# Linformer attention and an MLP mixer in one kernel: stores moved to GpSimd's queue, zero products in TensorE's early waits, another order of the first loads, and new turns between loads and DMA transposes

## The chip, the cores and the metric

The kernel runs on one core of one Trainium2 chip. The metric is the device time of one execution in microseconds (us); the smaller is the better. Before the change it was 439.4 us, the median of four runs (438.73 to 440.3 us). When the prediction was made, three of these were known, with a median of 438.74 us.

TensorE is the engine of the matrix products, VectorE (DVE in the profile) and ScalarE (ACT) do elementwise work, GpSimd (POOL) does elementwise work and issues DMAs, and SyncE (SP) only issues DMAs here.

## The reference, cut to what matters

```python
# batch 8, heads 8, sequence 1024, head width 64; E and F are 64 x 1024
k_proj = einsum('ks,bhsd->bhkd', E, k)
v_proj = einsum('ks,bhsd->bhkd', F, v)
attn   = softmax(q @ k_proj^T / 8)            # 1024 x 64 per head
x      = attn @ v_proj                        # then heads side by side: 8 x 1024 x 512
h      = relu(x^T @ w_tok1) @ w_tok2          # token mixing, 1024 -> 256 -> 1024
u      = x + h^T
out    = u + relu(u @ w_ch1) @ w_ch2          # channel mixing, 512 -> 1536 -> 512
```

Channel mixing is most of the work. The kernel does it with seven products of half-size blocks instead of eight, so it needs u transposed (called `uT`, two halves per batch: `uT0` and `uT1`), sums of blocks of `uT` (called `S`), and combinations of weight blocks (`wT`).

## The kernel before

The program gives every piece of work to a planner written in Python, as a job with an engine, an estimated duration, dependencies and a priority. The planner simulates the engines and lays down the order in which jobs are emitted. On the chip each engine then runs its jobs in that order and waits where an input is missing. The parts which the change and the argument touch follow; cuts are marked.

The start: the first batch's loads, pair of heads by pair of heads, with the two token-mixing weights near the end. All loads are issued by GpSimd, so they stand in one in-order queue.

```python
    for hp in range(HP):                       # HP = 4 pairs of heads
        if hp == HP - 1:
            ...
            ld(1.05, dma(wt1_sb, w1t), writes=["wt1"], prio=next(first))
        for name in "kvq":
            load_heads(0, name, 2 * hp, 2, next(first))
    ...
    ld(1.05, dma(wt2_sb, w2t), writes=["wt2"], prio=next(first))
    # ... then the channel weights, then batch 1
    for i in range(8):
        warm(i)                                # eight products of zeros, one per PSUM bank
```

The steady part: DMA transposes of q and u and all stores are issued by SyncE. The loads of the next batch are issued behind a transpose (`tie` makes one DMA wait for another), so that loads and transposes take turns.

```python
    def q_transpose(due):                      # qT <- q_sb, two DMA transposes on SyncE
        for h in range(0, H, H // 2):
            before = turned[0]
            turned[0] = sp(3.5, lambda h=h: nc.sync.dma_start_transpose(...), ...)
            if before:
                turned[0].deps.add(before)
    ...
            j = sp(3.5, lambda: nc.sync.dma_start_transpose(out=uT_t[i]..., in_=u_t[b % 2]...), ...)
            if landed[0]:
                tie(j, landed[0])              # uT waits for the last load issued
            turned[0] = j
    ...
        def store(sh):                         # two stores per block, sixteen blocks
            sp(1.5, lambda: nc.sync.dma_start(out=out_v[b, :, rows, :], in_=o_t[os[sh]]), ...)
    ...
    def load_batch(b):                         # k, v and q of batch b, all together
        jobs = [load_heads(b, n, hh, H // 2, None) for n in "kvq" for hh in range(0, H, H // 2)]
        for j in jobs if turned[0] else ():
            tie(j, turned[0])                  # behind the last transpose
        landed[0] = jobs[-1]
```

The softmax here doesn't subtract the row's maximum and nothing guards it: scores larger than these inputs give would overflow.

Of the kernel before, what the change touches and what calls it, by code (L numbers as in the profile page):

```python
# [10 lines left out]
BF16 = mybir.dt.bfloat16  # L11
ALU = mybir.AluOpType
ACT = mybir.ActivationFunctionType
FMAX = 3.4028234663852886e38


# [18 lines left out]
class Planner:  # L35
# [4 lines left out]
    def __init__(self, caps, homes):  # L40
        self.jobs, self.caps, self.homes = [], caps, homes
        self.wrote, self.readers = {}, {}

    def add(self, eng, occ, lat, fn, reads=(), writes=(), prio=None, takes=(), uses=(), after=()):
        j = Job(len(self.jobs), eng, occ, lat, fn, prio)
# [26 lines left out]
    def plan(self):  # L72
# [2 lines left out]
                d.next.append(j)  # L75
        for j in reversed(self.jobs):
            if j.prio is None:
                due = [s.prio for s in j.next]
                j.prio = (min(due) if due else 1e9) - j.occ - 0.3
        for j in self.jobs:  # L80
            if j.prio > 1e8:
                j.prio = max((d.prio for d in j.deps), default=0) + 2
# [3 lines left out]
        est = {}  # L86
# [39 lines left out]
        while any(can.values()):  # L126
            pick = None
            for e, js in can.items():
                f = free.get(e, 0.0)
                cands = []  # L130
                for j in js:
                    t = max(f, est[j.n])
                    spot = None
                    if j.takes:
                        h = home(j.takes[0], t)
                        if h is None:
                            continue
                        t, spot = h[0], h[3]
                    cands.append((t, j.prio, j.n, j, spot))
                if not cands:  # L140
                    continue
                t0 = min(c[0] for c in cands) + 0.02
                c = min((c for c in cands if c[0] <= t0), key=lambda c: (c[1], c[2]))
                if pick is None or c[0] < pick[0]:
                    pick = c
            if pick is None:
                raise RuntimeError("no job can go on", [(j.eng, j.fn.__qualname__, j.prio) for js in can.values() for j in js][:20], held, bank_free)
            t, _, _, j, spot = pick
            can[j.eng].remove(j)
            j.start, j.end, j.full = t, t + j.lat, t + j.lat + 0.03  # L150
            free[j.eng] = t + j.occ
            if j.takes:
                b = j.takes[0]
                b.at = spot
                turn[b.stream].remove(b)
                held[b.stream] += 1
                bank_free[spot] = None
            for b in j.banks:
                left[id(b)] -= 1
                if not left[id(b)]:  # L160
                    held[b.stream] -= 1
                    bank_free[b.at] = max(x.end for x in b.jobs) + 0.1
                    clean[b.at] = b.full
            order.append(j)
            for s in j.next:
                waiting[s.n] -= 1
                if not waiting[s.n]:
                    open_(s)
        assert len(order) == len(self.jobs), (len(order), len(self.jobs))
        return order  # L170


@with_exitstack
def kernel(
# [14 lines left out]
    P = 128  # L189
# [139 lines left out]
            writes=[(name, i) for i in range(h, h + hn)], prio=due,  # L329
        )  # L330
    first = iter(range(-1000, 0))
    for hp in range(HP):
        if hp == HP - 1:
            w1t = moe_w_tok1.rearrange("(p si) t -> p si t", p=P)
            ld(1.05, dma(wt1_sb, w1t), writes=["wt1"], prio=next(first))
        for name in "kvq":
            load_heads(0, name, 2 * hp, 2, next(first))
    w2t = moe_w_tok2.rearrange("(tc p) s -> p tc s", p=P)
    ld(1.05, dma(wt2_sb, w2t), writes=["wt2"], prio=next(first))
    w1_v = moe_w_ch1.rearrange("(dc p) (ch c) -> p dc ch c", p=P, ch=2)  # L340
    cw = DC // 2 // SETS
    for m in range(SETS):
# [32 lines left out]

    def blank(b):
        nc.tensor.matmul(  # L377
            b, zero, vb.rearrange("k h c d -> k (h c d)")[:, 0:S2], start=True, stop=True
        )

    def warm(i):
# [10 lines left out]
        make_identity(nc, ident)  # L392
        make_identity(nc, ident32)

    pl.add("POOL", 1.0, 1.0, identities, writes=["ident"], prio=-150)

    for n, (src, dst) in enumerate(((EF[0], ET_sb), (EF[1], FT_sb))):
        b = Bank("F", full=False)

        def view(b=b):  # L400
            return bank(b).rearrange("p (si k) -> p si k", si=NSI)

        def turn(src=src, view=view):
            for si in range(NSI):
                nc.tensor.transpose(view()[:, si, :], src[:, si:S:NSI], ident32)

        def take(dst=dst, view=view):
            nc.vector.tensor_copy(out=dst, in_=view())

        pl.add("PE", 1.6, 1.6, turn, reads=["ident"], takes=[b], prio=-150)  # L410
        dve(512, take, writes=["ET", "FT"][n : n + 1], uses=[b], prio=-150)

    def combine(T, b11, b12, b21, b22, cols, name, n, reads):
        def one(k, out, in0, in1, *deps):
# [93 lines left out]
            writes=[("kT", 1, h) for h in heads], uses=[bk],  # L508
        )

    turned = [None]
    landed = [None]

    def q_transpose(due):
        for h in range(0, H, H // 2):
            before = turned[0]
            turned[0] = sp(
                3.5,
                lambda h=h: nc.sync.dma_start_transpose(
                    out=qT[:, h : h + H // 2].rearrange("p h j s -> p (h j) s"),  # L520
                    in_=q_sb[:, h : h + H // 2].rearrange("p h si d -> p (h si d)"),
                ),
                reads=[("q", i) for i in range(h, h + H // 2)],
                writes=[("qT", i) for i in range(h, h + H // 2)], prio=due,
            )
            if before:
                turned[0].deps.add(before)

    def q_transpose_pe(hp, due):
        bk = Bank(stream[0], full=False)  # L530
# [93 lines left out]
    def token2(b, si, due):  # L624
# [20 lines left out]
        if si % NJ == NJ - 1:  # L645
            i = si // NJ
            j = sp(
                3.5,
                lambda: nc.sync.dma_start_transpose(
                    out=uT_t[i].rearrange("p s dc q -> p (s dc) q"),  # L650
                    in_=u_t[b % 2][:, i * NJ : (i + 1) * NJ].rearrange("p s d -> p (s d)"),
                ),
                reads=[("u", b % 2, n) for n in range(i * NJ, (i + 1) * NJ)],
                writes=[("uT", i, n) for n in range(HP)], prio=None,
            )
            if landed[0]:
                tie(j, landed[0])
            turned[0] = j

    def quarter(j, sh, dh):  # L660
        return uT_t[j % 2][:, 2 * sh : 2 * sh + 2, 2 * dh : 2 * dh + 2, :]
# [1 line left out]
    def s_sums(j):  # L663
        St = S_t[j % 2]
        a11, a12, a21, a22 = [quarter(j, sh, dh) for sh in range(2) for dh in range(2)]
        rd = [("uT", j % 2, n) for n in range(HP)]

        def one(n, in0, in1, add=False, deps=()):
            f = nc.vector.tensor_add if add else nc.vector.tensor_sub
            dve(  # L670
                512, lambda: f(out=St[:, n], in0=in0, in1=in1), ps=False,  # L671
                reads=rd + [("S", j % 2, m) for m in deps], writes=[("S", j % 2, n)],
            )

        one(0, a21, a22, add=True)
        one(2, a11, a21)
        one(1, St[:, 0], a11, deps=(0,))
        one(3, a12, St[:, 1], deps=(1,))

# [191 lines left out]
    def down_block(j):  # L871
# [30 lines left out]
        def product(n, i):  # L902
# [5 lines left out]
            for t in range(2):  # L908
# [5 lines left out]
                    prio=due_d(j, 2 * i + t),  # L914
                )

        def store(sh):
            rows = slice(i * NJ + 2 * sh, i * NJ + 2 * sh + 2)
            sp(
                1.5, lambda: nc.sync.dma_start(out=out_v[b, :, rows, :], in_=o_t[os[sh]]),  # L920
                reads=[o_key(sh, 0), o_key(sh, 1)], prio=None,
            )

# [52 lines left out]
            u_transpose_pe(hp, i, (-5.5 if i == 0 else 1.5) + 0.5 * hp)  # L976
    stream[0] = "F"

    def load_batch(b):
        jobs = [load_heads(b, n, hh, H // 2, None) for n in "kvq" for hh in range(0, H, H // 2)]  # L980
        for j in jobs if turned[0] else ():
            tie(j, turned[0])
        landed[0] = jobs[-1]

    def front(b, begin, end):
        units = []
# [5 lines left out]
        for i in range(H // hn):  # L992
            unit(1.9 * hn / H, lambda t, i=i: kv_proj(b, i * hn, hn, t))
            unit(0.9 * hn / H, lambda t, i=i: k_transpose(i * hn, hn, t))
            if b == 1:
                for hp in range(2 * i, 2 * i + 2):
                    unit(0.4, lambda t, hp=hp: q_transpose_pe(hp, t))
        unit(0.4, lambda t: scores(0, t))
        unit(0.4, lambda t: scores(1, t))
        for h in range(H):  # L1000
            if h + 2 < H:
                unit(0.4, lambda t, h=h: scores(h + 2, t))
            for half in range(2):
                unit(0.25, lambda t, h=h, half=half: attend(h, half, t))
        if b + 1 < B:
            unit(0.0, lambda t: load_batch(b + 1))
        for n in range(TC):
            unit(1.8, lambda t, n=n: token1(n, t))
        for si in range(NSI):
# [10 lines left out]
    for b in range(B):  # L1020
# [5 lines left out]
        if b + 1 < B:  # L1026
            at = 2 * TU * (b + 1)
            if b > 0:
                q_transpose(None)
            front(b + 1, at - 62, at - 14)  # L1030
    gate = mybir.DependencyInfo(mybir.DependencyClass.Sync, mybir.DependencyReason.DATA)
    plan = pl.plan()
    name_of = {}
    shown = None
    for j in plan:
        n = len(nc.cur_bb.bb.instructions)
        j.fn()
        new = nc.cur_bb.bb.instructions[n:]
# [35 lines left out]
```

## Time and profile before

| what | reading | view |
|---|---|---|
| device time | 439.4 us, median of 4 | times |
| span of the profiled execution | 439.5 us (its device time was 441.52 us) | page |
| TensorE busy | 418.5 us, 95% | page |
| TensorE idle, 45 to 420 us | 4.7 us | windows |
| TensorE at half pace | from 9.3 until about 22 us | timeline, spacing of equal products |
| DMA transpose of u, issue to landing | 4.3 / 4.6 / 7.2 us (min / median / max) | tile uT, 60 to 440 us |

The first lines are from the page of the kernel before: the busy times of the engines, and the shares of the chain that ended last.

```profile
PE 418.5 (95%) x3736; PEld 338.4 (77%) x3736; DVE 321.0 (73%) x783; ACT 241.1 (55%) x439; POOL 106.2 (24%) x122
PE 86%; DVE 7%; ACT 2%; DMA 2%; issue 1%; DVEq 0%; ACTq 0%
```

TensorE bounds this kernel: it is busy for 95% of the span and holds 86% of the chain.

The windows of the kernel before show it by stage. The columns are the stretch, its length, then the busy time and number of instructions of PE, PEld, DVE, ACT and POOL, the granted TensorE clock, the mean busy share of the DMA engines (it may exceed 1 where packets overlap), and GB/s.

```profile
0.00:22.90 22.90, 15.98 (x122) 10.16 (x122) 8.52 (x31) 8.84 (x17) 15.47 (x28) 1.00 1.08 188
22.90:45.00 22.10, 19.96 (x260) 17.20 (x261) 17.11 (x51) 14.39 (x30) 7.54 (x10) 1.00 1.31 203
45.00:165.00 120.00, 118.50 (x1075) 96.02 (x1074) 99.30 (x252) 72.60 (x132) 27.58 (x30) 1.00 0.86 155
165.00:420.00 255.00, 251.83 (x2178) 204.81 (x2177) 190.23 (x443) 141.41 (x255) 51.04 (x50) 1.00 0.62 123
420.00:439.50 19.50, 12.19 (x108) 10.24 (x105) 5.87 (x11) 3.84 (x7) 4.57 (x4) 0.97 0.27 108
```

From 45 to 420 us TensorE is idle for 1.5 + 3.2 us. The room is in the first 45 us, where the DMA engines are saturated (share above 1) and TensorE waits for data.

The next lines are TensorE's timeline of the kernel before: start, duration, engine, line, operation, output and inputs. They are two equal pairs of projection products at two moments, and the first product that needs the first batch's `uT` of the last pair of heads.

```profile
9.29 0.31 PE L455 MATMUL ps<-k_sb,ET_sb 128*64 128x128 bf16 x1
9.40 0.31 PE L455 MATMUL ps<-k_sb,ET_sb 128*64 128x128 bf16 x1
25.91 0.22 PE L455 MATMUL ps<-k_sb,ET_sb 128*64 128x128 bf16 x1
25.96 0.22 PE L455 MATMUL ps<-k_sb,ET_sb 128*64 128x128 bf16 x1
38.91 0.60 PE L801 MATMUL ps<-uT,wc_sb 128*128 128x256 bf16 x4
```

Equal products start 0.11 us apart at 9.3 us and 0.05 us apart at 25.9 us: early on TensorE runs at half pace. The clock column of the windows says 1.00 for that stretch, so it does not show this; the spacing of equal products does. The Trainium skill, "TensorE: Matmul & The Clock Gate", Part 1 (The HAM clock gate), has the mechanism: a gate lets half of the clock pulses through until TensorE has been active for a whole window of about 3.4 us. The trace agrees with the factor of two.

Last, three views of how u transposes fare in the kernel before: the waits in SyncE's queue (line, what it waited for, us in total, times, longest), the landing line of tile `uT`, and the one landing of a u transpose among the longest pieces of the chain (start, us, what).

```profile
SPq L920 <- POOL o L927: 189.0, 13, 67.4
SPq L649 <- DVE u L640: 62.4, 7, 18.2
```

```profile
DMA to landing us min/median/max: 4.3/4.6/7.2
```

```profile
269.21 7.15 DMA uT<-u
```

The stores (L920) wait in SyncE's queue for GpSimd's addition, and the transposes (L649) wait 62.4 us for u itself, which is as it should be; of their other waits, 43.5 us end with TensorE's products and 32.6 us with VectorE's G (lines not shown). Once issued, a transpose needs 4.3 to 7.2 us, and only one of them lies on the chain with its landing.

### The profile page before, as it was taken

How to read it: one execution, taken by the hardware profiler on the slowest of the kernel's cores; microseconds unless marked ns; L12 is line 12 of the kernel's file. 1: busy time of each engine (PE TensorE's matmuls, PEld its weight loads, DVE VectorE, ACT ScalarE, POOL GpSimd, SP SyncE). 2: the span in 40 equal slices, each digit the busy share in tenths (PEclk: the TensorE clock that was granted, in tenths of full speed). 3: DMA queues.
4: the chain of work that ended last, by engine and by line, in shares of the span. 5: the costliest groups of instructions: out<-in, count | busy, mean ns of one | idle time of the engine just before them, and what ended most of it. 6: DMA issues, size and time to landing. Idle time of an engine off the chain costs nothing.

```text
span 439.5 us, 9315 instructions
## 1 busy us (share of the span) xinstructions
PE 418.5 (95%) x3736; PEld 338.4 (77%) x3736; DVE 321.0 (73%) x783; ACT 241.1 (55%) x439; POOL 106.2 (24%) x122
## 2 busy tenths in 40 slices
PE   6789999999999999999999999899999999999993
PEld 4468888578778886788778877688768886888883
DVE  3459969678978797779697696778697596966451
ACT  1557786258536754567356654558436663555540
POOL 8442123032301331115021331115112210212212
PEclk9999999999999999999999999999999999999999
DMA  9999979289955899198955899187992811241022
GB/s 167 208 199 207 206 123 195 91 186 167 177 94 152 126 194 172 46 224 149 197 89 120 139 189 203 22 193 140 199 142 47 195 48 49 50 145 61 36 98 95
DMA packets 89516, 60.89 MB, mean 139 GB/s; under 512 B 55681, under 2 KB 84865, under 8 KB 89473
## 3 DMA queue, kind: packets, MB, share of 16 engines
q0 software_dynamic: 30624, 29.36, 42.7%
q1 hardware_dynamic: 58768, 30.68, 29.4%
q8 instruction: 29, 0.48, 0.4%
q10 hardware_dynamic: 80, 0.26, 0.3%
q14 instruction: 15, 0.11, 0.1%
HBM read 59.24 MB, written 16.78 MB: 173 GB/s over the span
## 4 chain that ended last, share of the span: by engine, by line
PE 86%; DVE 7%; ACT 2%; DMA 2%; issue 1%; DVEq 0%; ACTq 0%
PE ps L896 32%; PE ps L801 30%; PE ps L609 6%; PE ps L629 5%; PE ps L555 3%; PE ps L455 3%; PE ps L578 3%; DMA uT<-u 2%; DVE S L671 1%; DVE u L728 1%; PE ps L539 1%; ACT qT L547 1%; PE ps L377 1%; PE ps L689 1%; DVE da L943 1%
## 5 line engine op out<-in xcount | busy, mean ns | idle before, releaser
L896 PEld LDWEIGHTS <-G 128*128 128x128 bf16 x1344 | 130.0, 98 | 24.5 <-issue 5.7
L896 PE MATMUL ps<-wc_sb,G 128*128 128x256 bf16 x768 | 103.8, 273 | 3.9 <-DVE da L943 2.7
L801 PEld LDWEIGHTS <-wc_sb 128*128 128x128 bf16 x768 | 73.6, 98 | 14.3 <-issue 1.6
L823 ACT ACTIVATE G<-ps 128x512 bf16<-128x512 f32 x96 | 57.2, 599 | 39.9 <-PE ps L801 39.6
L896 PE MATMUL ps<-wT,G 128*128 128x256 bf16 x576 | 77.7, 272 | 0.1
L927 POOL TENSOR_TENSOR o<-o,u 128x512 f32<-128x512 f32 x32 | 37.4, 1169 | 130.3 <-ACT o L925 115.2
L801 PEld LDWEIGHTS <-wT 128*128 128x128 bf16 x576 | 55.1, 98 | 11.2 <-issue 2.2
L801 PE MATMUL ps<-uT,wc_sb 128*128 128x256 bf16 x384 | 57.6, 273 | 0.0
L801 PE MATMUL ps<-S,wc_sb 128*128 128x256 bf16 x384 | 57.6, 273 | 0.0
L927 POOL TENSOR_TENSOR db<-db,u 128x512 f32<-128x512 f32 x16 | 18.9, 1182 | 157.5 <-ACT db L925 157.5
L801 PE MATMUL ps<-S,wT 128*128 128x256 bf16 x384 | 54.9, 273 | 0.9 <-ACT G L823 0.7
L640 DVE TENSOR_TENSOR u<-ps,x_sb 128x512 bf16<-128x512 f32 x56 | 35.7, 684 | 22.2 <-PE ps L629 21.7
L595 DVE TENSOR_TENSOR x_sb<-ps,rdn 128x256 bf16<-128x256 f32 x128 | 49.7, 415 | 0.3
L836 DVE TENSOR_TENSOR G<-G 128x512 bf16<-128x512 bf16 x96 | 46.7, 489 | 3.4
L782 DVE CUSTOM_DVE_ANT_0 g<-ps,ub 128x512 bf16<-128x512 f32 x48 | 32.8, 684 | 20.4 <-PE ps L801 20.3
L782 DVE CUSTOM_DVE_ANT_0 G<-ps,ua 128x512 bf16<-128x512 f32 x48 | 32.7, 682 | 18.1 <-ACT ua L829 18.0
L564 ACT ACTIVATE a<-ps 128x512 bf16<-128x512 f32 x64 | 37.1, 600 | 12.4 <-PE ps L555 12.2
L829 ACT COPY ua<-ps 128x512 f32<-128x512 f32 x48 | 28.1, 586 | 24.2 <-PE ps L801 23.6
L829 ACT COPY ub<-ps 128x512 f32<-128x512 f32 x48 | 28.1, 586 | 9.6 <-PE ps L801 9.2
L842 ACT COPY ps<-ps 128x512 f32<-128x512 f32 x48 | 28.3, 589 | 6.9 <-DVE g L782 4.2
L578 PE MATMUL ps<-vb,a 128*128 128x130 bf16 x256 | 30.9, 226 | 0.6 <-DVE x_sb L595 0.6
L629 PE MATMUL ps<-hT_sb,wt_sb 128*128 128x512 bf16 x112 | 29.5, 379 | 0.0
(69 smaller groups left out, 521.7 us busy)
## 6 DMA issues: line engine op xcount, KB each, us to landing
out_dram<-o SPq DMA_DIRECT2D x32, 512.0 KB, 3.6
k_sb<-in_k_dram POOLq DMA_DIRECT2D x14, 512.0 KB, 8.6
v_sb<-in_v_dram POOLq DMA_DIRECT2D x14, 512.0 KB, 13.0
q_sb<-in_q_dram POOLq DMA_DIRECT2D x14, 512.0 KB, 9.9
wc_sb<-in_moe_w_ch_dram POOLq DMA_DIRECT2D x6, 256.0 KB, 12.9
wc_sb<-in_moe_w_ch_dram POOLq DMA_DIRECT2D x4, 384.0 KB, 12.1
k_sb<-in_k_dram POOLq DMA_DIRECT2D x4, 256.0 KB, 6.7
v_sb<-in_v_dram POOLq DMA_DIRECT2D x4, 256.0 KB, 7.2
```

The source lines that it names most:

```text
L564: lambda: nc.scalar.activation(out=a_t[h % 4], in_=bank(bk), func=ACT.Exp, scale=scale),
L578: nc.tensor.matmul(view()[:, 2 * jj : 2 * jj + 2].rearrange("p c d -> p (c d)"), a_t[h % 4][:, j * P : (j + 1) * P], vb[:, h].rearrange("k ...
L595: lambda: nc.vector.tensor_tensor(out=x_sb[:, 4 * half : 4 * half + 4, h * D : (h + 1) * D], in0=view()[:, :, 0:D], in1=rdn[:, :, None].to ...
L629: nc.tensor.matmul(bank(bk), wt2_sb[:, t, si::NSI], hT_sb[:, t, :], start=(t == 0), stop=(t == TC - 1),)
L640: lambda: nc.vector.tensor_add(out=u_t[b % 2][:, si, :], in0=bank(bk), in1=x_sb[:, si, :]),
L782: nc.vector._custom_dve(TENSOR_ADD_SAT, out=out, in0=in0, in1=in1, s0=FMAX, s1=0.0)
L801: nc.tensor.matmul(t[:, c, :], w1_of(n, dd, 2 * m + c), a_of(j, n, dd), start=(n in (1, 7) and c == 0 and dd == 0), stop=(c == 1 and dd == 1),
L823: lambda: nc.scalar.activation(out=G[:, n, cs], in_=view(src), func=ACT.Relu),
L829: 512, lambda: nc.scalar.copy(out=dst, in_=view("y")), writes=[(name, s % 2)],
L836: 512, lambda: f(out=G[:, n, cs], in0=in0, in1=in1), ps=False, reads=deps,
L896: nc.tensor.matmul(view(X_OF[n])[:, t, :], G[:, G_OF[n], cc, t * P : (t + 1) * P], w2_of(n, cc), start=(n in (1, 7) and t == 0 and cc == 0 ...
L927: 512, lambda: nc.gpsimd.tensor_add(out=dst, in0=dst, in1=u_of(sh, dh)),
```

## The change

Its intent is threefold. TensorE's early waits are filled with more products of zeros, so that its clock gate opens sooner, and token mixing gets its weights earlier, so that real work fills those waits too. The stores leave SyncE's queue to the transposes. And the loads of q go out separately from those of k and v, each behind a transpose, and earlier. The diff, cut to its core:

```diff
+LOADS = "01tT23"                          # pairs 0, 1, then both token weights, then pairs 2, 3
...
-    for hp in range(HP):
-        if hp == HP - 1:
+    for step in LOADS:
+        if step == "t":
             ld(1.05, dma(wt1_sb, w1t), writes=["wt1"], prio=next(first))
...
-            nc.vector.tensor_copy(out=dst, in_=view())
+            (nc.scalar.copy if n else nc.vector.tensor_copy)(out=dst, in_=view())
...
+    turned_u = {}
+    def q_transpose(b, behind):
...
+        if b + 1 < B:
+            last = load_group(b + 1, "q", j)          # q of the next batch behind the q transposes
+            if b > 2:
+                tie(turned_u[b - 1, 0], last)         # uT0 behind these loads
...
-            if landed[0]:
-                tie(j, landed[0])
-            turned[0] = j
+            turned_u[b, i] = j
...
-        one(0, a21, a22, add=True)
         one(2, a11, a21)                              # the first S sum needs half of uT only
+        one(0, a21, a22, add=True)
...
+        queue = nc.gpsimd if j < NSB - 1 else nc.sync
...
-                1.5, lambda: nc.sync.dma_start(out=out_v[b, :, rows, :], in_=o_t[os[sh]]),
+                1.5, lambda: queue.dma_start(out=out_v[b, :, rows, :], in_=o_t[os[sh]]),
...
+    def load_kv(b):
+        last = load_group(b, "kv", turned_u.get((b - 2, 0)))   # k, v behind uT0 of batch b-2
+        if (b - 2, 1) in turned_u:
+            tie(turned_u[b - 2, 1], last)                      # uT1 behind these loads
...
+        return sorted(order, key=lambda j: j.at)               # emission by ready time
...
+        if j.eng == "PE":                                      # zeros in planned waits
+            for _ in range(int((j.start - idle - 0.3) / 0.216) if spare is not None else 0):
+                blank(spare)
```

Counting batches from zero, it leaves the q loads of batch 3 (the fourth) without a turn against `uT0` of batch 1 (the second).

## The prediction

> **What bounds the kernel now.** TensorE: busy 95% of the 439.5 us span (page), 86% of the chain of waits. The table of windows: 45 to 420 us, only 4.7 us idle; after 420 us, 7.3 us idle, mostly the drain of the last store. Only the start is loose. From 0 to 22.9 us TensorE is busy 15.98 us, but at half pace (timeline): 128-column products of the projection are 105 ns apart, 54 ns from 25.8 us on. The granted-clock row says 1.00 all along, so this is no throttle. The Trainium skill, "TensorE: Matmul & The Clock Gate", Part 1, has a gate that opens after about 3.4 us of sustained activity; the trace agrees with its factor of two, but opened only near 22.9 us. The first product that needs the last pair's uT comes at 38.9 us.
>
> The load queue is saturated from 3 to 60 us (DMA share 1.2, about 205 GB/s). By the waits of GpSimd's issues head pair 1 has landed at 13.0 us, pair 2 at 16.9, the first token weight 19.4, pair 3's q 24.3, the second token weight 26.7. Token mixing bunches at 30 to 39 us.
>
> **What the change does.**
> 1. Token weights load behind pair 1: by the same rate at about 15.5 and 18 us; pair 2 at 21.7, pair 3 at 26.7 (2.4 later). Same bytes. Mixing of pairs 0 and 1 runs while TensorE now waits (build order).
> 2. Fourteen more zero products (22, not 8), 0.43 us each at half pace, 0.22 at full, to fill waits; the gate should open between 7 and 14 us. One cast of the projection weights (0.69 us) goes to ScalarE.
> 3. Stores but the last block's go to GpSimd's queue: about 0.75 us of issue each (as its loads take), 28 times, on an engine 24% busy. SyncE's queue is left to transposes, which stood behind stores; one u transpose took 7.2 us to land (median 4.6), on the chain at 269 us.
> 4. Loads of q, and of k and v, go out separately and earlier.
>
> **On the critical path.** Start: by 26.7 us TensorE had done about 9.5 us of work in full-pace time (estimate from product counts and pitches); after, the work available by then is about 14.8 us. Some of these 5.3 us are lost again in pair 3's latency chain (about 9 us). Estimate: 3.5 us earlier, that first product near 35 us. From there TensorE is saturated, so the gain is kept. Middle: of 4.7 us idle, about 1.7 recovered. End: nothing. 438.7 − 3.5 − 1.7 = 433.5 us.
>
> **Predicted** 433.5 us, 8 in 10 between 429.5 and 437.5. Faster by over 2% (below 430): 0.12; within 2%: 0.85; slower: 0.03.
>
> **Right or wrong if:** the 105 ns pitch ends before 14 us; the first product on the last pair's uT moves from 38.9 to about 35; TensorE's idle from there to the last block falls from 4.7 to about 3; no transpose wait on the chain near 270 us; its busy time from 45 us on is otherwise unchanged.
>
> **What would make it wrong:** zero products placed by a plan delay real work where the wait is shorter than planned (two more precede the first weight transposes); GpSimd's in-order queue puts additions behind loads and stores that wait, so buffers and PSUM banks come free late; batch 1's loads, landing until 60 us, become the limit; the gate stays shut.

## The result, and the profile after

The changed kernel took 446.75 us, the median of four runs (445.54 to 447.37 us), with correct results. The ratio to the kernel before is 1.0163, with a 95% interval of 1.0131 to 1.0195. It is slower by 1.6%, and outside the predicted range of 429.5 to 437.5 us. Here and below a ratio is the mean time of one kernel's runs over that of the other's in the same rounds, so it is not quite the ratio of the medians that are quoted.

The page of the changed kernel has these lines for busy times and chain.

```profile
PE 422.2 (95%) x3750; PEld 337.4 (76%) x3750; DVE 318.9 (72%) x782; ACT 243.4 (55%) x440; POOL 122.8 (28%) x152
PE 80%; DMA 8%; DVE 7%; ACT 3%; issue 1%; DVEq 0%; ACTq 0%
```

TensorE's share of the span is the same 95%, which says nothing. The chain says more: DMA's share went from 2% to 8%. Eight per cent of 444.9 us is 36 us of chain that a DMA now holds; much of it runs beside other work that would have ended almost as late, so it is not a loss of 36 us.

The windows of the changed kernel have the same columns as before.

```profile
0.00:22.90 22.90, 19.10 (x175) 11.63 (x177) 8.96 (x30) 8.35 (x17) 14.14 (x27) 1.00 1.06 187
22.90:45.00 22.10, 18.60 (x231) 14.76 (x226) 19.52 (x55) 15.77 (x33) 8.87 (x12) 1.00 1.32 202
45.00:165.00 120.00, 113.26 (x995) 88.92 (x994) 91.76 (x237) 68.67 (x124) 31.03 (x37) 0.99 0.98 172
165.00:420.00 255.00, 253.59 (x2206) 207.01 (x2204) 188.86 (x443) 143.76 (x257) 61.93 (x70) 1.00 0.54 115
420.00:444.90 24.90, 17.67 (x158) 15.12 (x155) 9.83 (x18) 6.87 (x13) 6.82 (x7) 0.95 0.22 85
```

Up to 22.9 us TensorE did 175 products, zeros included, where it did 122 before, and from there to 45 us 231, where it did 260: what it gained first it gave back. From 45 to 165 us it did 995 products, where it did 1075 before, and was idle for 6.7 us, where it was 1.5. From 165 us to 420 us it lost even less than before (1.4 against 3.2 us idle). So the loss sits between 45 and 165 us, and the gain of the first 23 us seems to be gone by 45 us.

A count of work makes both sharper. I added up, product by product, the real matrix work of each trace (each product of 256 columns at 0.109 us and of 128 at 0.055 us, the spacing at full pace; zeros not counted), and read when each kernel reaches equal amounts of it.

```
work done, us   before reaches it at   the changed kernel, us earlier (-) or later (+)
      2               12.41                +1.25
     12               30.30                -2.90
     26               46.63                -0.09
     64               83.23                -0.43
     72               91.61                +1.35
     88              108.65                +3.44
    128              147.60                +3.26
    136              155.62                +7.55
    240              257.72                +8.21
    320              338.09                +6.45
    end                                    +5.47
```

At 30 us the changed kernel leads by 2.9 us. At 46 us the lead is gone, before the steady part begins; against the execution of odd_stores_pool, with its faster start, the changed kernel is 1.5 us late there. Then it falls behind in three steps, near 90, 109 and 153 us, and gets back about 2 us later on, where the kernel before had small stalls of its own. The spans differ by 5.4 us, less than the medians (7.35 us), since the profiled execution of the kernel before was a slow one.

TensorE's timeline of the changed kernel shows the start.

```profile
10.84 0.31 PE L465 MATMUL ps<-k_sb,ET_sb 128*64 128x128 bf16 x1
10.95 0.31 PE L465 MATMUL ps<-k_sb,ET_sb 128*64 128x128 bf16 x1
13.73 0.22 PE L465 MATMUL ps<-k_sb,ET_sb 128*64 128x128 bf16 x1
13.79 0.22 PE L465 MATMUL ps<-k_sb,ET_sb 128*64 128x128 bf16 x1
38.50 0.73 PE L812 MATMUL ps<-uT,wc_sb 128*128 128x256 bf16 x4
```

The 0.11 us spacing ends between 11 and 13.7 us, so the gate did open before 14 us. But the product on the last pair's `uT` starts at 38.50 us, 0.4 us earlier than before, and not at 35 us.

The next lines are the timeline of the changed kernel around the three steps; SPq is SyncE's queue, and the bracket is the idle time before the instruction and what ended it.

```profile
82.09 2.25 SPq L662 DMA_TRANSPOSE uT<-u  x1
82.32 1.48 POOL L322 DMA_DIRECT2D q_sb<-in_q_dram  x2 [8.22 <-DMA qT<-q_sb]
83.78 0.56 POOL L934 DMA_DIRECT2D out_dram<-o  x1
90.62 0.60 PE L812 MATMUL ps<-uT,wc_sb 128*128 128x256 bf16 x4 [0.79 <-DMA uT<-u]
...
107.40 1.91 SPq L662 DMA_TRANSPOSE uT<-u  x1
111.89 0.27 PE L812 MATMUL ps<-uT,wc_sb 128*128 128x256 bf16 x1 [2.45 <-DMA uT<-u]
...
150.37 2.99 SPq L662 DMA_TRANSPOSE uT<-u  x1
154.68 0.43 DVE L682 TENSOR_TENSOR S<-uT 128x512 bf16<-128x512 bf16 x1 [2.71 <-DMA uT<-u]
155.50 0.32 PE L591 MATMUL ps<-vb,a 128*128 128x130 bf16 x2 [2.52 <-DVE x_sb L608]
```

At 82 us `uT0` goes out at 82.09 us, and two q loads and a store follow it within 1.7 us. At 107 and 150 us `uT1` goes out only there, since it has waited for the k and v loads, and TensorE stands for 2.45 and 2.52 us. The third stop reaches TensorE by way of VectorE, whose queue holds an S sum in front of the work that TensorE needs.

The window just after the third stop, the chain's landings of u transposes, the waits of SyncE's queue and the landing line of tile `uT`, all of the changed kernel, complete it.

```profile
155.00:160.00 5.00, 4.50 (x28) 3.49 (x28) 3.60 (x14) 1.17 (x2) 0.00 (x0) 0.66 1.06 197
```

```profile
82.09 8.49 DMA uT<-u
107.40 4.45 DMA uT<-u
150.37 4.28 DMA uT<-u
249.23 5.80 DMA uT<-u
```

```profile
SPq L662 <- DMA v_sb<-in_v_dram: 107.3, 5, 23.0
SPq L662 <- DVE u L653: 86.7, 8, 30.1
```

```profile
DMA to landing us min/median/max: 4.2/4.4/8.5
```

After the stop of 2.52 us the granted clock is 0.66 over five microseconds: (1 - 0.66) x 5 / 0.5 = 3.4 us at half pace, which costs 1.7 us more. That is why the third step in the table is about 4.3 us and not 2.5. The transpose at 82 us took 8.49 us, and the transposes now wait 107.3 us in all for the last load of v, a wait that the kernel before did not have among its largest.

### The profile page after: what moved, and what is told of

The parts are those of the page before. It is cut to its first block, busy times and chain, and to the rows that moved or that the text cites. A ratio compares the mean times of both kernels' runs of the same rounds, so it can differ in the third digit from the quotient of the medians. Undisturbed runs are those within 1.5% of the kernel's fastest.

```text
span 444.9 us, 9354 instructions
## 1 busy us (share of the span) xinstructions
PE 422.2 (95%) x3750; PEld 337.4 (76%) x3750; DVE 318.9 (72%) x782; ACT 243.4 (55%) x440; POOL 122.8 (28%) x152
## 4 chain that ended last, share of the span: by engine, by line
PE 80%; DMA 8%; DVE 7%; ACT 3%; issue 1%; DVEq 0%; ACTq 0%
PE ps L812 29%; PE ps L907 28%; DMA uT<-u 8%; PE ps L622 5%; PE ps L642 5%; PE ps L465 3%; PE ps L591 2%; PE ps L568 2%; DVE x_sb L608 2%; PE ps L387 2%; ACT qT L560 1%; DVE S L682 1%; DVE wT L426 1%; ACT a L577 1%; DVE G L847 1%
## 5 line engine op out<-in xcount | busy, mean ns | idle before, releaser
L907 PE MATMUL ps<-wc_sb,G 128*128 128x256 bf16 x768 | 104.9, 274 | 2.3 <-DVE da L957 0.9
L608 DVE TENSOR_TENSOR x_sb<-ps,rdn 128x256 bf16<-128x256 f32 x128 | 51.2, 418 | 0.9
L847 DVE TENSOR_TENSOR G<-G 128x512 bf16<-128x512 bf16 x96 | 44.5, 465 | 3.9 <-DVE G L847 0.5
L653 DVE TENSOR_TENSOR u<-ps,x_sb 128x512 bf16<-128x512 f32 x56 | 38.0, 686 | 10.9 <-PE ps L642 10.6
L840 ACT COPY ua<-ps 128x512 f32<-128x512 f32 x48 | 28.2, 588 | 22.9 <-PE ps L812 22.4
L591 PE MATMUL ps<-vb,a 128*128 128x130 bf16 x256 | 32.0, 221 | 4.6 <-DVE x_sb L608 3.5
L642 PE MATMUL ps<-hT_sb,wt_sb 128*128 128x512 bf16 x112 | 32.7, 379 | 0.0
```

What stands on the lines that cost most here:

```text
L591: nc.tensor.matmul(view()[:, 2 * jj : 2 * jj + 2].rearrange("p c d -> p (c d)"), a_t[h % 4][:, j * P : (j + 1) * P], vb[:, h].rearrange("k ...
L608: lambda: nc.vector.tensor_tensor(out=x_sb[:, 4 * half : 4 * half + 4, h * D : (h + 1) * D], in0=view()[:, :, 0:D], in1=rdn[:, :, None].to ...
L642: nc.tensor.matmul(bank(bk), wt2_sb[:, t, si::NSI], hT_sb[:, t, :], start=(t == 0), stop=(t == TC - 1),)
L653: lambda: nc.vector.tensor_add(out=u_t[b % 2][:, si, :], in0=bank(bk), in1=x_sb[:, si, :]),
L840: 512, lambda: nc.scalar.copy(out=dst, in_=view("y")), writes=[(name, s % 2)],
L847: 512, lambda: f(out=G[:, n, cs], in0=in0, in1=in1), ps=False, reads=deps,
```

## Experiments

Fourteen kernels ran, each correct unless I say so, and each beside the kernel before on the same chip. The letters in the quoted expectations stand for theories. T: the new turns between loads and transposes, and their clashes, cost the time. S: the stores in GpSimd's queue cost it. P: the lead of the start is lost since the last pair of heads lands 2.3 us later. V: it is lost since VectorE is the limit between 33 and 45 us. C: a store and a u transpose in flight together hinder each other.

| kernel | median us | ratio to before | 95% interval |
|---|---|---|---|
| the change | 446.75 | 1.0163 | 1.0131 to 1.0195 |
| stores_sync | 457.63 | 1.0393 | 1.0351 to 1.0435 |
| no_turn_kv | 446.46 | 1.0140 | 1.0103 to 1.0178 |
| no_zeros | 446.29 | 1.0136 | 1.0097 to 1.0175 |
| loads_as_before | 443.01 | 1.0051 | 1.0008 to 1.0093 |
| q_behind_u | 440.79 | 1.0021 | 0.9988 to 1.0055 |
| q_behind_u_old_loads | 436.83 | 0.9950 | 0.9888 to 1.0013 |
| q_behind_u_kv_turn | 441.38 | 1.0027 | 0.9990 to 1.0064 |
| before_stores_pool | 448.59 | 1.0206 | 1.0164 to 1.0248 |
| odd_stores_pool | 439.16 | 0.9980 | 0.9954 to 1.0005 |
| before_new_start | 438.58 | 0.9966 | 0.9932 to 0.9999 |
| pair3_in_time | 439.78 | 0.9997 | 0.9966 to 1.0029 |
| short_combines | 439.79 | 0.9997 | 0.9974 to 1.0019 |
| all_turns | 435.84 | 0.9922 | 0.9889 to 0.9955 |
| kv_behind_u | 436.98 | 0.9925 | 0.9902 to 0.9949 |

### stores_sync: the change, with the stores back in SyncE's queue

```diff
-        queue = nc.gpsimd if j < NSB - 1 else nc.sync
+        queue = nc.sync
```

> The changed kernel with all stores back in SyncE's queue; plan and order of every compute engine are the same. Theory T (turns): the time is lost because the second u transpose of a batch now waits until the k and v loads of a later batch have landed (it started 0.08 us after the last v load landed at 107.32 us and 0.13 us after it at 150.24 us), so this edit changes little: 445 to 448 us, both TensorE stalls of about 2.5 us (near 109 and 153 us) stay. Theory S (stores): stores in GpSimd's in-order queue hold up the loads behind them; then this gets most of the 7 us back, to 439 to 442 us, and the two stalls go.

It took 457.63 us, 11 us more than the change: both expectations missed. The order of the computing instructions is the same, so the queue alone did this. The trace shows how. The numbers are times of issue, of landing, the engine and what was moved.

```
stores in SyncE's queue                     the change
187.12  202.37  GpSimd  v                   187.74  199.90  GpSimd  v
192.82  200.82  SyncE   store               193.69  201.16  GpSimd  store
194.04  202.53  SyncE   store               194.90  202.47  GpSimd  store
202.42  208.56  SyncE   uT1                 200.04  204.32  SyncE   uT1
```

The last v load took 15.2 us beside stores of another queue, and 12.2 us where the stores stood behind it in its own. `uT1` must wait for that load by the new turns, so it went out 2.4 us later. TensorE had four stops of 2.3 us or more after 100 us (4.06, 3.61, 2.59 and 2.30 us), where the change has two. Given these turns, moving the stores was right, and S as the cause of the loss falls.

### no_turn_kv: `uT1` does not wait for the k and v loads

```diff
-            tie(turned_u[b - 2, 1], last)
+            turned_u[b - 2, 1].deps.add(last)   # the planner's order only, no wait on the chip
```

> The changed kernel, where the second u transpose of a batch no longer waits for the k and v loads to have landed; the plan and the order on all engines are the same, one semaphore wait is gone. Theory T: both stalls near 109 and 153 us go (3.1 us and 2.5 us plus 1.7 us of half pace), so about 6 us come back: 439 to 442 us. Theory S (stores) or a start that costs more: no change, 445 to 448 us.

It took 446.46 us, as the change did, where T had expected 439 to 442 us. The stops at 109 and 153 us were gone, but that at 90 us had grown to 4.17 us: the q loads of the fourth batch happened to go out 0.04 us before `uT0`, not after it, and `uT0` took 11.86 us. These are the first two landings of u transposes on the chain of this kernel.

```profile
81.93 11.86 DMA uT<-u
142.68 12.00 DMA uT<-u
```

One half of T (the wait) was worth as much as the other half (the clash) got worse. The run could not tell the sizes.

### no_zeros: the change without its fourteen added zero products

```diff
-            for _ in range(int((j.start - idle - 0.3) / 0.216) if spare is not None else 0):
+            for _ in range(0):
```

> The changed kernel with the fourteen added zero products not issued, all else in the same order. If zero products open the gate early: the half pace lasts until 18 us or later instead of 12.3 us, and the early lead over the kernel before (2.9 us at equal work near 27 us) shrinks to about 1.5 us. Theory V (VectorE limits 27 to 54 us, where it is busy without a break) says the lead is lost by 46 us anyway, so the time stays within 1 us of the changed kernel's 446.7. Theory Z (zero products in TensorE's way cost time): faster by 1 to 2 us.

It took 446.29 us: the added zeros are worth nothing measurable in the whole time of this kernel. They do keep the gate open: in the four traces of kernels without added zeros, products still ran at half pace at 15.5, 15.9, 21.7 and 21.7 us, and in the twelve with them no half pace shows between 12.1 and 40 us. The lines are windows of this kernel.

```profile
9.00:12.00 3.00, 2.18 (x32) 1.71 (x30) 0.85 (x3) 1.70 (x4) 1.81 (x3) 0.55 1.24 205
12.00:16.00 4.00, 3.81 (x36) 2.53 (x32) 1.60 (x9) 2.69 (x6) 1.67 (x3) 0.50 1.10 213
```

Without the added zeros the gate had opened near 5.7 us, closed again from 9.3 to 16.2 us (granted clock 0.50 to 0.55), not until 18 us as expected. The early lead did not shrink to 1.5 us either: it was 4.0 us at 30 us, where the change had 2.9 us, and 1.1 us at 46 us, where the five kernels with zeros and the same order of loads had 0.1 to 1.3 us. So half pace in this stretch cost nothing measurable; that TensorE lacked data there, and not pace, is the likely reason. The whole times alone would not show this, since the stop near 90 us was longer here (4.38 us, with 6.83 us of half pace behind it).

### loads_as_before: the change with the old order of the first loads

```diff
-LOADS = "01tT23"
+LOADS = "012t3T"
```

> The changed kernel with the old order of the first loads (pair 2, first token weight, pair 3, second token weight). Its plan is made anew, so the orders on the engines differ. Theory V (VectorE limits the stretch up to 54 us): the early lead near 27 us becomes smaller than 2.9 us, but at 46 us the kernel stands where the changed one does, within 0.7 us. Theory P (pair 3 landing 2.4 us later ate the gain): at 46 us it is 1 to 2 us ahead.

It took 443.01 us, 3.3 to 3.5 us less than the two kernels above. By the count of work it leads the kernel before by 3.52 us at 46 us, where the others lead by 0.24 to 1.16 us. P had expected 1 to 2 us there, so the effect is larger than expected. So the new order of loads costs what the start was to bring. P holds so far; V is not excluded by this run.

### q_behind_u and q_behind_u_old_loads: the clash at 82 us taken away

These are no_turn_kv, with the q loads of the fourth batch put behind `uT1` of the second; the second of them has the old order of the first loads as well.

```diff
-            last = load_group(b + 1, "q", j)
+            last = load_group(b + 1, "q", j if b > 2 else turned_u[1, 1])
```

> The changed kernel, with no wait of the second u transpose for the k and v loads, and with the q loads of the fourth batch (the ones at 82 us, which had no turn set against the first u transpose) issued only after both u transposes of the second batch. Theory C (contention: a u transpose that shares the DMA engines with loads lands in 8.5 to 11.9 us instead of about 4.4, and TensorE then waits): that u transpose lands within 6 us of issue, the stalls at 89, 109 and 153 us all shrink below 1 us, and the time is 438 to 441 us. If the stalls come from somewhere else (the plan's order, GpSimd's queue), 444 us or more.

> The kernel of the run before, with the old order of the first loads. The run with the old order alone was 2.4 us further at 46 us than runs of the same early gate. Theory P (pair 3 landing 2.4 us later ate the gain of the start) says the same here: 2 to 3 us under the run before, so 435.5 to 438.5 us, faster than both kernels. If the earlier difference came from another plan by chance: within 1 us of the run before.

They took 440.79 and 436.83 us, both within the expected ranges. From no_turn_kv to q_behind_u one missing turn is worth 5.7 us; from q_behind_u to the other, the order of the first loads is worth 4.0 us, more than the expected 2 to 3 us. By the traces 2.1 of these 4.0 us are there at 46 us (leads of 1.28 and 3.36 us); most of the rest arises between 83 and 109 us, under another plan. One thing in q_behind_u speaks for care: five of its `uT1` took 9.4 to 12.5 us to land, and yet TensorE never stood for more than 0.83 us. A slow landing costs only where TensorE has nothing else to do. One execution of the last took 441.41 us, where its others took 435.65 to 437.72 us; why is not known.

### q_behind_u_kv_turn: the clash taken away, the wait kept

```diff
-            last = load_group(b + 1, "q", j)
+            last = load_group(b + 1, "q", j if b > 2 else turned_u[1, 0])
```

> The changed kernel with one thing undone: the q loads of the fourth batch wait for the first u transpose of the second batch (near 82 us); the second u transposes still wait for the k and v loads. If the clash at 82 us is the root (the late transpose makes the k and v loads late, and these the next transposes): that transpose lands within 6 us, the stalls at 109 and 153 us go too, 440 to 442 us. If the wait for the k and v loads costs by itself: the stall at 153 us (2.5 us and 1.7 us of half pace) stays, 443 to 446 us.

It took 441.38 us. This is the change with nothing undone but the clash at 82 us, and it gets back 5.4 of the 7.35 us by the medians. The time is that of the first expectation, but only one of the two stops went. `uT0` landed 4.79 us after its issue. The wait of `uT1` for the k and v loads is still there, with a stop of 1.86 us at 150.68 us, without half pace after it. Compared with q_behind_u (440.79 us), that wait is worth 0.6 us by the medians and 2.2 us by the spans of the two profiled executions. They were run at other times.

### before_stores_pool and odd_stores_pool: the stores moved alone, in the kernel before

```diff
-                1.5, lambda: nc.sync.dma_start(out=out_v[b, :, rows, :], in_=o_t[os[sh]]),
+                1.5, lambda: (nc.gpsimd if j < NSB - 1 else nc.sync).dma_start(out=out_v[b, :, rows, :], in_=o_t[os[sh]]),
```

In odd_stores_pool the condition is `j % 2 and j < NSB - 1`: only the blocks whose stores don't fall beside a u transpose.

> The kernel before with the stores but the last block's in GpSimd's queue and nothing else changed (the plan is the same). If the move of stores is harmless or good by itself: 437.5 to 440.5 us, and SyncE's transposes start no later than before. If it costs by itself: GpSimd's additions wait behind stores, and the time is over 442 us.

> The kernel before with only the odd blocks' stores in GpSimd's queue (not the last block's); the even blocks' stores, which fall together with the second u transposes, stay in SyncE's queue, where the second of them cannot start before the transpose has been issued. Theory C (what the moved stores cost is their overlap with a u transpose): second u transposes land within 6 us of issue, 438.5 to 441.5 us. If GpSimd's own queue makes the cost (8.6 us for all 30 stores), about half of it stays: 443 to 446 us.

Moved alone, the stores cost 2.06% (448.59 us; the interval of the ratio reaches from 1.0164 to 1.0248). Moving the odd blocks' stores costs nothing (439.16 us); not all transposes landed within the expected 6 us there, but the longest (6.8 us) is as long as at the same place in the kernel before (6.78 us). The following lines are the landing line of tile `uT` and the longest landing of the chain in before_stores_pool, and then the landing line of odd_stores_pool.

```profile
DMA to landing us min/median/max: 4.3/5.6/11.1
288.84 11.10 DMA uT<-u
```

```profile
DMA to landing us min/median/max: 4.2/4.5/6.8
```

The same moment in the kernel before and in before_stores_pool (issue, landing, engine, what) tells why.

```
before                                      before_stores_pool
287.18  290.20  SyncE  store                288.84  299.94  SyncE   uT
287.62  294.40  SyncE  uT                   289.09  296.45  GpSimd  store
290.80  295.44  SyncE  store                289.66  299.93  GpSimd  store
```

In SyncE's queue the second store was issued only after the transpose had been issued in full, at 290.71 us, and it stayed mostly out of its way. In GpSimd's queue both stores went out within 0.9 us of the transpose, and it took 11.10 us, where it had taken 6.78 (a transpose of q followed it in both, after 3.8 and 2.8 us). The order of one queue had kept them apart without anyone having written it down.

### before_new_start: only the start's zeros, cast and S order, in the kernel before

The diff is cut: the edit also takes over the new S order, another PSUM bank for the first transposes, and one estimate of the planner. The plan then holds 18 added zeros, not 14.

```diff
+            for _ in range(int((j.start - idle - 0.3) / 0.216) if spare is not None else 0):
+                blank(spare)
...
+            (nc.scalar.copy if n else nc.vector.tensor_copy)(out=dst, in_=view())
```

> The kernel before with only the parts of the change that bear on the first 12 us (zero products in planned waits, one cast of the projection weights on ScalarE, the new order of the S sums), the old order of loads, old stores, old turns. If the early gate is worth something when nothing later takes it back: at 46 us of the kernel before this one is 2 to 4 us ahead, and ends at 435 to 438 us. If VectorE limits the stretch to 54 us: level with the kernel before at 54 us, and 438 to 440 us.

It took 438.58 us, a ratio of 0.9966 (0.9932 to 0.9999). The time lies in V's range, while the trace fits the other expectation: it leads the kernel before by 2.1 us at 46 us and by 2.5 us at the end, so with the old order of loads the lead is not lost. But 1.6 us of such a lead come from the slow start of that one profile (odd_stores_pool, with the start of the kernel before, leads it by as much at 46 us), so this run hardly bears on V. It shows how much a single profile may mislead here: 2.5 us in the traces, and about 1.5 us in the timed runs.

### pair3_in_time and short_combines: P against V

pair3_in_time is q_behind_u with `LOADS = "01t23T"`: the first token weight behind pair 1, the second after pair 3. short_combines is q_behind_u with the combinations of the weights cut to 16 columns, so that VectorE has less to do between 33 and 45 us; its result is wrong (relative error 0.70), and two buffers are cleared once at the start.

```diff
-                cols, lambda: nc.vector.tensor_sub(out=out, in0=in0, in1=in1), ps=False,
+                cols, lambda: nc.vector.tensor_sub(out=out[..., 0:16], in0=in0[..., 0:16], in1=in1[..., 0:16]), ps=False,
```

> The kernel q_behind_u with the second token weight loaded last (after pair 3) and the first one still behind pair 1, so that pair 3 lands when it does in the kernel before. Theory P (pair 3's late landing costs the start): at 46 us of the kernel before it is 3 to 4 us ahead instead of 1.3, and the time is 436 to 438.5 us. If the order of the first token weight were to blame, or VectorE: about q_behind_u's 440.8 us.

> The kernel q_behind_u with each of the 20 subtractions that make the combined channel weights cut to 16 columns (a wrong result on purpose; it takes about 6 us of VectorE's work out of 33 to 54 us). Theory V (VectorE limits that stretch): the lead over the kernel before, 4.1 us at 12 us of work, is kept at 46 us, and the time is 437 to 438.5 us. Theory P: TensorE waits for pair 3's chain all the same, the lead at 46 us stays at 1.3 to 2 us, and the time is 439.5 to 441.5 us.

pair3_in_time leads by 3.35 us at 46 us, as P said; the other changed kernels with pair 3 on time lead by 2.8 to 3.5 us. Its time, 439.78 us, missed the expectation: by its trace a `uT1` issued at 183.23 us took 13.01 us, and TensorE stood for 2.58 us at 195.8 us. A gain of the start was lost to a clash further on. By the trace this is the cause above at another place; no run took it away.

In short_combines VectorE was no longer full. The windows are those of q_behind_u and of short_combines, 33 to 39 and 39 to 45 us.

```profile
33.00:39.00 6.00, 4.56 (x59) 3.77 (x57) 5.97 (x15) 3.39 (x7) 2.51 (x4) 1.00 1.25 207
39.00:45.00 6.00, 5.53 (x46) 4.38 (x46) 5.93 (x14) 4.43 (x9) 0.46 (x1) 1.00 1.24 206
```

```profile
33.00:39.00 6.00, 5.01 (x64) 4.18 (x62) 5.04 (x18) 3.67 (x7) 2.47 (x5) 1.00 1.26 207
39.00:45.00 6.00, 5.44 (x47) 4.30 (x46) 3.86 (x13) 4.39 (x9) 0.62 (x1) 1.00 1.24 206
```

VectorE's busy time fell from 11.90 to 8.90 of 12 us, and the lead at 46 us went from 1.28 only to 1.59 us; the time is 439.79 against 440.79 us. They were run at other times. A full engine was not the limit: V falls, P stands.

### all_turns and kv_behind_u: what the experiments point to

all_turns is q_behind_u_old_loads, with the stores of even blocks made to wait for the `uT1` beside them. kv_behind_u puts the k and v loads behind `uT1` on top of it.

```diff
+            if i and b > 1:                       # at the issue of uT1
+                for sh in range(2):
+                    tie(stored[2 * b - 2, sh], j) # both kernels: stores behind uT1
...
-        last = load_group(b, "kv", turned_u.get((b - 2, 0)))
+        load_group(b, "kv", turned_u.get((b - 2, 1)))   # kv_behind_u only
```

> The best so far (q_behind_u with the old order of the first loads, 436.8 us) with the stores that fall together with the second u transposes made to wait for them. Theory C: second u transposes land within 6 us of issue, no TensorE stall over 1 us after 40 us, 435 to 437.5 us in all rounds (the run before had one at 441.4 us), so faster than the kernel before by about 0.8%.

> The kernel all_turns (435.84 us) with the k and v loads behind the second u transpose instead of the first, so that u transposes share the engines with no load or store. Theory C: all u transposes from the fourth batch on land within 6 us, no TensorE stall over 1 us, 434 to 436.5 us. If the k and v loads, now later, become the limit: stalls before a projection, over 438 us.

all_turns took 435.84 us (435.18 to 439.0 us in six runs), a ratio of 0.9922 (0.9889 to 0.9955). It beats both kernels. kv_behind_u took 436.98 us, a ratio of 0.9925 (0.9902 to 0.9949), so the two cannot be told apart, and neither can all_turns be told from q_behind_u_old_loads (436.83 us): what its added turn is worth is not shown. The next lines are the landing line of tile `uT` in all_turns and in kv_behind_u.

```profile
DMA to landing us min/median/max: 4.2/4.3/8.9
```

```profile
DMA to landing us min/median/max: 4.2/4.3/6.1
```

I had expected that every second transpose of all_turns lands within 6 us, and no run over 437.5 us; four of them took 7.2 to 8.9 us, a stop of 1.7 us near 156 us remained, and two runs took 437.77 and 439.0 us. In kv_behind_u all land within 6.1 us and no stop after 40 us is longer than 1.0 us, as expected, and yet it is not faster, and misses the expected 434 to 436.5 us. Why is not shown: no landing of a later k or v load is on its chain.

## Why the prediction was wrong

**What bounds the kernel** was right. TensorE's work is the floor in every variant, and its busy share is 95% before and after.

**"Estimate: 3.5 us earlier, that first product near 35 us. From there TensorE is saturated, so the gain is kept."** This step failed. The gate opened before 14 us, as predicted, and the lead was 2.9 us at 30 us. But the pair of heads that lands last sets the end of the start. Its q landed at 26.34 us, where it had landed at 24.05 us before, since both token weights now go ahead of it; the product on its `uT` came at 38.50 us, not near 35 us, and the lead at 46 us was 0.1 us. The prediction had this delay in it ("2.4 later") and set it against a pool of 5.3 us of work as "some" that is lost again. That was the error: work done early from other pairs does not shorten the chain that hangs from the last arrival. With the old order of loads the lead at 46 us is 3.4 to 3.5 us, and the time is 3.4 us (loads_as_before) to 4.0 us (q_behind_u_old_loads) shorter. So the part of the change that was named as the first source of gain is a cost. The estimate had a second fault: it was read from a profile whose start was slow, and taken off a median of faster executions. Against the start of odd_stores_pool even the kernels with the old order lead by only 1.7 to 1.9 us at 46 us, and the changed kernel is 1.5 us late.

**"Middle: of 4.7 us idle, about 1.7 recovered."** This step failed too, with the opposite sign: the changed kernel lost about 8 us between 83 and 156 us, and got back about 2 of them later. From 45 to 420 us TensorE's idle time rose from 4.7 to 8.1 us, and a stretch of half pace came on top, where a fall to about 3 us was predicted. The prediction listed that the loads "go out separately and earlier" and gave this no cost. What the runs showed in its place is a clash: two q loads and a store issued within 1.7 us of a u transpose double its landing from 4.3 to 8.5 us (and to 11.86 us where a load was ahead of it). With this one clash taken away the change takes 441.38 us: it accounts for 5.4 us. The new wait of `uT1` for the k and v loads accounts for 0.6 us by the medians, 2.2 us by the traces.

**"Stores ... SyncE's queue is left to transposes, which stood behind stores."** The mechanism was half right, and the step has no single sign. Alone, the move costs 2.06%, because the shared queue had kept the second store away from the transpose. Under the new turns it saves 11 us, because stores in another queue slow the loads for which the transposes wait. The predicted issue times did not show as a cost: a store's issue took 0.53 to 0.60 us of GpSimd, not 0.75 (there are 30 such stores, not 28), and odd_stores_pool, which moves half of them, is no slower than the kernel before. The Trainium skill, "DMA: Bandwidth & Descriptors", section "Issuing engines are not separate DMA queues", says that all DMAs run on the same 16 engines and interleave, whatever engine started them, and that several issuers only save issue time. The first half agrees with these traces. The second does not cover what was measured: the choice of the issuer decided which DMAs overlap, and moved the time by +2% in one kernel and by -11 us in the other.

**The zeros** do what they were to do with the gate, and are worth nothing measurable in the time of this kernel (446.29 us without them, 446.75 us with them).

**A stop can cost twice.** After the stop of 2.52 us at 153 us TensorE ran for 3.4 us at half pace. The Trainium skill, "TensorE: Matmul & The Clock Gate", section "Why this matters for your kernels", puts the limit at gaps of about 3 us. Here the gate closed after stops of 2.30 and 2.52 us, and not after stops of 2.45, 2.59 and 3.29 us (the last in before_stores_pool, at 300 us). That the window runs free of the kernel, as Part 1 of that page states, would explain this; half-pace stretches of 3.41 us or 6.83 us, one or two windows, agree with it, but no run here set the window's phase on purpose.

**The end** stayed as it was, as predicted, and the loads of batch 1 did not become the limit (TensorE was busy for 14.99 of the 15 us from 45 to 60 us).

The two causes add up: undoing the order of loads alone gains 3.7 us by the medians (446.75 to 443.01 us), undoing the turns alone 6.0 us (to 440.79 us), and undoing both gains 9.9 us (to 436.83 us), where the sum is 9.7.

What stays open: the effects of emission by ready time and of the new S order were not isolated; every edit shifts the planner's schedule, so that single terms are good to 1 or 2 us; and why some executions of the best kernels took 2 to 5 us longer (439.0 and 441.41 us) is not known. How often the gate of the kernel before opens as late as about 22 us is known only by inference: that profile lists a mean clock of 0.999, since its early half pace has no record, and odd_stores_pool, which has the record, 0.991. Of the 36 timed executions of the kernel before that list a clock, 10 have 0.996 or more (median 440.5 us) and 26 have 0.992 or less (median 439.8 us).

## What to carry to other kernels

An order that several DMAs get from standing in one queue may be a turn that nobody wrote down: before you move DMAs to another queue, look at what they will overlap there, and write the turn down as a dependency. Judge a DMA on the chain by its time from issue to landing, not by engine busy shares: it went from 4.3 to 8.5 or 12 us here while TensorE's 95% did not move. Then ask whether TensorE stood still for it: in q_behind_u five landings of 9.4 to 12.5 us cost no stop above 0.83 us. Before you estimate a gain from a profile, compare its own time with the median of the timed runs. A gain in the start of a kernel survives only if the last input to arrive does not arrive later.

## What the Trainium skill lacked or had wrong

- "DMA: Bandwidth & Descriptors", section "DMA Transpose (X-bar)", has no figure for a transpose that shares the DMA engines with other transfers; its "Rules for kernel authors" say that a transpose next to ordinary DMAs needs nothing, which holds for correctness only. Here it took 4.3 us alone, 8.49 us beside two loads and a store, 11.10 us beside two stores and a transpose of q behind it, and 13.75 us at worst (in pair3_in_time).
- The same page, section "Issuing engines are not separate DMA queues", says that several issuing engines only save issue time. It gives no figure for what it is worth that the DMAs of one in-order issue queue go out one after the other (other sections of the page describe the order within a queue, not its price): with all else equal, moving the stores changed the time by +2.06% in the kernel before (ratio 1.0206), and moving them back changed it by +11 us in the changed kernel (446.75 to 457.63 us).
- "TensorE: Matmul & The Clock Gate", section "Why this matters for your kernels", advises against gaps above about 3 us. In these runs the gate closed after gaps of 2.30 and 2.52 us, and stayed open after 2.45, 2.59 and 3.29 us.
- "TensorE: Matmul & The Clock Gate", section "Seeing it yourself", warns that the records of the gate may be unreliable, but not that the half pace before the first record can be missing altogether: the clock row says 1.00 up to 22.9 us in the kernel before, while equal products start 0.11 us apart there and 0.05 us apart later.
